# A routed mixture of experts behind attention: spreading the later lists' work over other hooks, and one-hot rows on GpSimd

## The chip, the cores and the metric

The kernel runs on one core of a Trainium2 chip. A core has five engines with an instruction stream each: TensorE (PE, matrix products and transposes), VectorE (DVE), ScalarE (ACT), GpSimd (POOL) and SyncE (SP, which here issues the loads). They share SBUF; products accumulate in PSUM, which has eight banks here. Every engine works through its own list in order and waits on semaphores for the others. The metric is the device time of one execution in microseconds (us).

## The reference

Eight batches of 544 tokens (512 local and 32 global) go through attention with 8 heads of 64, and the outputs of all heads are joined to rows of 512, which go through a mixture of 8 experts:

```python
mask = np.abs(pos[:, None] - pos[None, :]) <= 32
s_ll = np.where(mask, scale * q_l @ k_l.T, -1e9)         # a local token sees its window and the global ones
a_l = sm(np.concatenate([scale * q_l @ k_g.T, s_ll], axis=-1))
out_l = a_l @ np.concatenate([v_g, v_l])                 # a global token sees all
...
for b in range(B):
    prev_e = -1
    for s in range(S):
        fresh_e = int(np.argmax(logits[b, s]))
        if s == 0 or local_gate[b, s] < 0.5:
            e = fresh_e
        else:
            e = prev_e if prev_e >= 0 else fresh_e       # a token may keep its predecessor's expert
        prev_e = e
        p = softmax(logits[b, s])
        out[b, s] = p[e] * (np.maximum(x[b, s] @ w1[e], 0) @ w2[e])
```

w1 is 512x1024 and w2 1024x512 for each expert. Which tokens an expert gets is known only once the attention of all batches is done.

## The kernel before

**Two parts that overlap.** Attention runs unit by unit over the eight batches. Then come the expert blocks of up to 256 or more tokens. Three *early blocks* (0, 1, 2) take tokens of the first batches, whose lists are ready while the last three batches' attention and routing still run; eight *rem blocks* follow, one for each expert, each with a Switch over cases of its token count; then full blocks under an If. The early blocks are the place of this change.

**An early block** (`early`) is 24 steps: eight chunks of the first layer (`mm1`: 12 products of 128x256 by PE, then relu and high half hh by ACT, L1276, then the low half hl by DVE, L1279), then eight chunks of the second layer for the first 128 tokens (j0) and eight for the second (j1) (`mm2`: three products of 128x512 each, L1287). Matrices are split into a high and a low half of a rounded format, and a product is made of three: high by high, low by high, high by low. Three PSUM banks rotate among the chunks of `mm1` here: a chunk can start only once hh and hl have been made of the chunk that last used its bank.

**Hooks.** After each of the 24 steps `hook(i, k)` runs. It takes one step of the *tail*, a generator with what remains of attention and routing (`Attn.tail`): the last units' transposes and value products (`g_t`, `g_av`, `l_t`, `l_av`), the finishing pieces f1 to f4, the expert keys, the ranks and lists, `kinds` (which makes cnd, the case of each rem block), and `rest` (products and picks for the remaining lists). Then it flushes: the low halves of weight pieces that ACT has cast (L1183, by DVE, 128x1024). Then it splits as many further pieces as the table SP says for this hook (ACT's cast, L1173). A freed buffer starts the next load. So the order of the code is the order of the work on each engine, and the number of yields sets at which hook a step falls. `every(g, n)` puts n steps of g in one hook, `lag(n)` lets n hooks pass.

**Ranks and lists.** `rank1` compares tokens with experts (oh), makes prefix sums (pc), and lets PE count over partitions (L875 to L884, into PSUM). `place` makes counts, bases and limits from that. `rank2` makes a token's position, and splits it in a low part of seven bits (plo) and a high part. `low` (L916) makes, for some chunks of 128 tokens, rows of 128 that are one at a token's low part, by comparing an iota with plo. `pick` makes three DVE operations for each group (L1000, L1002, L1004, tile xT: one-hots of the high parts and their two multiples, called *products* below), and then PE multiplies the two one-hots over all 34 chunks (L1010) to get the lists of token numbers. Those feed the gathers (indirect DMAs by POOL, L1214), and the gathered rows are transposed (`xpose`: PE L1228, ACT L1230, DVE L1231).

**The hint.** Ahead of the fifth j0 chunk of block 2, `hint` makes every engine load cnd (L1487) to prepare the first rem block's branch.

The lines around the change:

```python
        for _ in range(SP[i][k]):        # hook: the pieces that are split here
            self.split()
...
            if mid and fc == 4:          # early block 2, second layer
                self.finish(True)
                while not self.known:
                    self.take(next(self.tail))
                self.hint(i + 1)
```

Of the kernel before, what the change touches and what calls it, by code (L numbers as in the profile page):

```python
# [8 lines left out]
F32 = mybir.dt.float32  # L9
# [4 lines left out]
ALU = mybir.AluOpType  # L14
AX = mybir.AxisListType
PSUM = bass.MemoryType.PSUM
ENGS = (mybir.EngineType.PE, mybir.EngineType.Activation, mybir.EngineType.DVE, mybir.EngineType.Pool, mybir.EngineType.SP)

P = 128
# [11 lines left out]
NT = 34  # L31
NA = 5
CA = 4 * NA + 1
# [23 lines left out]
RE = 2  # L57
# [13 lines left out]
def lag(n):  # L71
    for _ in range(n):
        yield


def every(g, n):
    for k, _ in enumerate(g):
        if k % n == n - 1:
            yield
# [22 lines left out]
class Attn:  # L102
# [431 lines left out]
    def tail(self, sg, sl, fin, rt, moe):  # L534
        b = B - 1
        fin = [x for x in fin if x[0] is not None]
        self.g_t(sg)
        yield
        self.g_av(sg)
        self.at2.close()  # L540
        moe.alloc_a()
        yield
        self.l_t(sl, 0)
        self.l_t(sl, 1)
        yield
        self.l_av(sl, 0)
        yield
        self.l_av(sl, 1)
        self.at1.close()
        moe.alloc_b()  # L550
        yield
        while fin:
            f, a = fin.pop(0)
            f(*a)
            yield
        self.f1g(b)
        yield
        self.f1(b, 3)
        yield
        self.f2g(b)  # L560
        yield
        self.f2(b)
        yield from lag(2)
        self.f3(b, rt, False)
        yield
        c = self.cur[b]
        yield from every(rt.keys(b, c["L"]), 2)
        yield
        yield from rt.stage_b(self.ps_t, self.ps_o, rt.probs(b, c["L"], c["xa"]))
        self.f4(b, rt)  # L570
        yield from every(rt.lists(self.ps_o), 2)
        yield LISTS
        yield from every(rt.kinds(), 3)
        yield KINDS
        yield from every(rt.rest(self.ps_o), RE)


class Consts:
# [22 lines left out]
class Route:  # L601
# [4 lines left out]
    def setup(self):  # L606
        nc, cst, c = self.nc, self.cst, self.pool
# [32 lines left out]
        self.pos = c.tile([P, NT], F32, name="pos")  # L640
        self.pi = c.tile([P, 2, NT], I32, name="pi")
        self.plo = c.tile([P, NT], BF16, name="plo")
        self.o1 = c.tile([P, NT, P], BF16, name="o1")
        self.oe = c.tile([P, CA, 2, 2 * NX], BF16, name="oe")
        self.idx = c.tile([P, 2 * NX + 4 * E + 2 * NR], I32, name="idx")
# [214 lines left out]
    def rank1(self, c0, c1, po, first):  # L860
        nc = self.nc
        n = c1 - c0
        bc = [P, E, n]
        oh = self.oh[:, :, c0:c1]
        nc.vector.tensor_tensor(out=oh, in0=self.io8.rearrange("p (e o) -> p e o", o=1).broadcast_to(bc), in1=self.ei[:, c0:c1].rearrange("p (o t) -> p o t", o=1).broadcast_to(bc), op=ALU.is_equal)
        yield
        pcf = self.pc.rearrange("p e t -> p (e t)")[:, 0:E * n]
        pc = pcf.rearrange("p (e t) -> p e t", t=n)
        yield from self.prefix(oh, pc, n)
        if first:  # L870
            nc.vector.tensor_copy(self.sumA, pc[:, :, n - 1])
            yield
        else:
            cp = po()
            nc.tensor.matmul(cp[:, 0:E], self.ones, self.sumA, start=True, stop=False, skip_group_check=True)  # L875
            nc.tensor.matmul(cp[:, 0:E], self.ones, pc[:, :, n - 1], start=False, stop=True, skip_group_check=True)
            self.cntp = cp[:, 0:E]
        yield PSUM
        rp = po()
        rpv = self.rpv = rp[:, 0:E * n].rearrange("p (e t) -> p e t", t=n)  # L880
        nc.tensor.matmul(rpv, self.nlt, oh, start=True, stop=False, skip_group_check=True)
        if not first:
            nc.tensor.matmul(rpv, self.ones, self.sumA.rearrange("p (e o) -> p e o", o=1).broadcast_to(bc), start=False, stop=False, skip_group_check=True)
        nc.tensor.matmul(rpv, self.ones, pc, start=False, stop=True, skip_group_check=True)  # L884

    def rank2(self, c0, c1):
        nc = self.nc
        n = c1 - c0
        oh = self.oh[:, :, c0:c1]
        rv = self.rv.rearrange("p e t -> p (e t)")[:, 0:E * n].rearrange("p (e t) -> p e t", t=n)  # L890
        nc.vector.tensor_tensor(out=rv, in0=self.rpv, in1=oh, op=ALU.mult)
        yield
        nc.vector.tensor_reduce(out=self.pos[:, c0:c1], in_=rv.rearrange("p e t -> p t e"), axis=AX.X, op=ALU.add)
        yield
        nc.vector.tensor_copy(self.pi[:, 0, c0:c1], self.pos[:, c0:c1])
        yield
        nc.vector.tensor_scalar(out=self.pi[:, 1, c0:c1], in0=self.pi[:, 0, c0:c1], scalar1=7, scalar2=None, op0=ALU.arith_shift_right)
        yield
        nc.vector.tensor_scalar(out=self.pi[:, 0, c0:c1], in0=self.pi[:, 0, c0:c1], scalar1=127, scalar2=None, op0=ALU.bitwise_and)
        yield  # L900
        nc.vector.tensor_copy(self.plo[:, c0:c1], self.pi[:, 0, c0:c1])
        yield

    def prefix(self, oh, pc, n):
# [111 lines left out]
    def lists(self, po):  # L1016
        nc = self.nc
        yield from self.place(self.cntp, NT, NX, NR)
        cid = self.tmp("cid", [P, 2 * E + NR, 2], BF16)
        cr = cid[:, 0:2 * E].rearrange("p (e a) j -> p e (a j)", a=2)  # L1020
        cf = cid[:, 2 * E:]
        rm = self.tmp("rm", [P, E], I32)
        nc.vector.tensor_scalar(out=rm, in0=self.cn, scalar1=255, scalar2=None, op0=ALU.bitwise_and)
        yield
        sh = self.tmp("sh", [P, E], F32)
        nc.vector.tensor_scalar(out=sh, in0=self.left, scalar1=0.0, scalar2=None, op0=ALU.is_ge)
        yield
        nc.vector.scalar_tensor_tensor(out=sh, in0=rm, scalar=float(P), in1=sh, op0=ALU.is_le, op1=ALU.mult)
        yield
        fb = self.tmp("fb", [P, E], F32)  # L1030
        nc.vector.scalar_tensor_tensor(out=fb, in0=self.nbc, scalar=-4.0, in1=sh, op0=ALU.add, op1=ALU.subtract)
        yield
        nc.vector.tensor_tensor(out=cr, in0=fb.rearrange("p (e o) -> p e o", o=1).broadcast_to([P, E, 4]),
                                in1=self.io8[:, 0:4].rearrange("p (o j) -> p o j", o=1).broadcast_to([P, E, 4]), op=ALU.add)
        yield
        nc.vector.scalar_tensor_tensor(out=cr[:, :, 0], in0=sh, scalar=4.0, in1=fb, op0=ALU.mult, op1=ALU.add)
        yield
        ge = self.ge[:, NX:]
        mf = self.tmp("mf", [P, NR, E], F32)
        nc.vector.tensor_tensor(out=mf, in0=ge[:, :, 0:E], in1=self.sd.rearrange("p (o e) -> p o e", o=1).broadcast_to([P, NR, E]), op=ALU.mult)  # L1040
        yield
        k3 = self.tmp("k3", [P, NR], F32)
        nc.vector.scalar_tensor_tensor(out=k3, in0=self.ek, scalar=2.0, in1=self.k2[:, 0:NR], op0=ALU.mult, op1=ALU.add)
        yield
        m3 = self.tmp("m3", [P, NR], F32)
        nc.vector.tensor_reduce(out=m3, in_=mf, axis=AX.X, op=ALU.add)
        yield
        yield from self.rank2(CA, NT)
        nc.vector.scalar_tensor_tensor(out=cf[:, :, 0], in0=k3, scalar=-2.0, in1=m3, op0=ALU.add, op1=ALU.add)
        yield  # L1050
        phi = self.tmp("phi", [P, NT], BF16)
        nc.vector.tensor_tensor(out=phi, in0=self.hi, in1=self.pi[:, 1], op=ALU.add)
        yield
        nc.vector.tensor_scalar(out=cf[:, :, 1], in0=cf[:, :, 0], scalar1=1.0, scalar2=None, op0=ALU.add)
        yield
        for c0 in range(CA, NT, 5):
            yield from self.low(c0, min(c0 + 5, NT))
        self.pk = (cid, phi)
        yield from self.pick(cid, phi, self.o2, 0, 4, 2 * NX, ((0, NT),), po, 16)

# [33 lines left out]
class Moe:  # L1094
# [216 lines left out]
    def hook(self, i, k):  # L1311
# [9 lines left out]
        if i == NX - 1:  # L1321
            self.finish()
        for _ in range(SP[i][k]):
            self.split()
# [204 lines left out]
def _sp(d):  # L1529
    return [d.get(k, 0) for k in range(24)]  # L1530


SP = [_sp({1: 1, 2: 1, 3: 1, 4: 1, 6: 1, 7: 1, 10: 1, 13: 1, 15: 1, 19: 1}),
      _sp({0: 1, 1: 1, 2: 1, 3: 1, 5: 1, 7: 1, 8: 1, 11: 1, 13: 1, 15: 1, 17: 1, 19: 1}),
      _sp({1: 1, 3: 1, 5: 1, 7: 1, 10: 1, 12: 1, 14: 1})]


@with_exitstack
# [83 lines left out]
```

## Time and profile before

| what | value |
|---|---|
| median of 3 runs | 685.71 us (684.99 to 685.96) |
| the profiled execution's time | 684.55 us |
| its span | 682.8 us, so 1.75 us lie around the span |
| granted TensorE clock, mean | 0.995 |
| busy: PE, DVE, ACT, POOL | 655.4, 433.7, 342.1, 195.0 us |
| the chain that ended last, PE's share | 56% |

A row of the timeline gives start, duration, engine, line, operation, tiles (output <- inputs, buffer numbers left out), shape, and a count where several follow each other; in brackets stands the idle time of the engine ahead of it and what ended that. A DVE row can reach over the start of the next (a low half starts at 307.21, lasts 1.22, and the next row starts at 308.35), so DVE work in a row is priced by the distance of its starts. The early blocks lie between about 229 and 322 us of the span; lines of `kernel.py` before the change are meant everywhere.

### The profile page before, as it was taken

What the parts mean: (1) busy time and instruction counts of PE and PEld (TensorE: products, weight loads), DVE (VectorE), ACT (ScalarE), POOL (GpSimd) and SP (SyncE); (2) the same over time, 40 slices, a digit from 0 to 9 for tenths busy, and PEclk for the clock granted to TensorE, in tenths of its full rate; (3) what the DMA queues carried; (4) which work ended last, traced back from release to release, by engine and by line L of the source; (5) the groups of instructions that cost most, each with busy time, mean ns of one, the idle gap of its engine ahead of it and who ended that gap; (6) DMA issues with size and microseconds to landing.
All of it is one profiled execution on the core that took longest, in us unless ns stands there. A gap on an engine that the chain in (4) does not pass through costs nothing.

```text
span 682.8 us, 18511 instructions
## 1 busy us (share of the span) xinstructions
PE 655.4 (96%) x7285; PEld 556.2 (81%) x7285; DVE 433.7 (64%) x1101; ACT 342.1 (50%) x614; POOL 195.0 (29%) x321
## 2 busy tenths in 40 slices
PE   8999999999999899998999899999999999999995
PEld 7778778777677787886987798989898989898994
DVE  7878778788887677988425553626374526355573
ACT  4555556555555574743427534435354425255563
POOL 7634334343324301031213304021123011133023
PEclk9999999999999999999999999999999999999998
DMA  8966967866757497766626674528283617265673
GB/s 321 405 217 249 336 216 305 316 247 237 303 188 291 135 353 255 259 206 200 254 89 223 212 246 151 183 82 265 86 297 120 235 63 236 93 218 182 222 276 102
DMA packets 42886, 151.47 MB, mean 222 GB/s; under 512 B 7837, under 2 KB 9117, under 8 KB 38560
## 3 DMA queue, kind: packets, MB, share of 16 engines
q1 hardware_dynamic: 35536, 126.92, 52.5%
q0 software_dynamic: 6832, 21.90, 9.5%
q8 instruction: 78, 1.28, 0.8%
q14 instruction: 152, 1.25, 0.6%
q10 hardware_dynamic: 288, 0.13, 0.1%
HBM read 130.55 MB, written 19.16 MB: 219 GB/s over the span
## 4 chain that ended last, share of the span: by engine, by line
PE 56%; DVE 6%; issue 1%; ACT 1%; POOL 0%; DVEq 0%; POOLq 0%; ACTq 0%
PE ps L1274 26%; PE ps L1287 23%; PE ps L1228 2%; PE ps L1293 2%; DVE wp L1183 1%; DVE wq L1183 1%; DVE xT L1002 0%; DVE xT L1000 0%; PE ps L1010 0%; DVE xl L1183 0%; ACT wp L1173 0%; DVE wp L1231 0%; POOL xa L1214 0%; DVE o L916 0%; DVE xl L1231 0%
## 5 line engine op out<-in xcount | busy, mean ns | idle before, releaser
L1306 POOL DMA_INDIRECT out_dram<-y,tk x39 | 40.8, 1045 | 309.5 <-ACT y L1305 221.7
L1287 PE MATMUL ps<-wp,wq 128*128 128x512 f32 x444 | 114.5, 403 | 1.0 <-ACT wq L1403 1.0
L1274 PE MATMUL ps<-wp,wp 128*128 128x256 f32 (+6 forms) x672 | 107.7, 320 | 0.0
L1274 PEld LDWEIGHTS ps<-wp,wp 128*128 128x128 f32 x672 | 103.5, 188 | 3.5
L1287 PEld LDWEIGHTS ps<-wp,wq 128*128 128x128 f32 x444 | 82.2, 190 | 18.1 <-ACT wq L1403 1.2
L1279 DVE SCALAR_TENSOR_TENSOR wq<-ps,wq 128x384 fp32r<-128x384 f32 (+4 forms) x112 | 43.5, 414 | 56.5 <-ACT wq L1276 48.0
L193 POOL TENSOR_SCALAR_AFFINE_SELECT qbd<-raw 64x512 f32<-64x512 f32 x62 | 44.3, 714 | 118.4 <-PE ps L246 92.2
L1276 ACT ACTIVATE wq<-ps 128x256 fp32r<-128x256 f32 (+6 forms) x80 | 36.9, 463 | 76.0 <-PE ps L1274 63.9
L246 PE MATMUL ps<-kx,qbd 128*64 128x128 f32 x1024 | 67.4, 275 | 1.3 <-issue 0.7
L1231 DVE TENSOR_TENSOR wp<-ps,wp 128x512 fp32r<-128x512 f32 x40 | 27.5, 691 | 58.3 <-ACT wp L1230 58.3
L257 ACT ACTIVATE pe<-pe 128x512 f32<-128x512 f32 x64 | 40.7, 636 | 43.8 <-DVE pe L253 43.8
L246 PEld LDWEIGHTS ps<-kx,qbd 128*64 128x64 f32 x1024 | 58.5, 138 | 2.1 <-POOL kx L193 1.1
L251 DVE TENSOR_REDUCE mx<-ps 128x4 f32<-128x512 f32 x64 | 43.8, 685 | 24.3 <-PE ps L246 24.1
L1183 DVE TENSOR_TENSOR wp<-raw,wp 128x1024 fp32r<-128x1024 f32 x47 | 57.0, 1217 | 2.9 <-ACT wp L1173 2.8
L1214 POOL DMA_INDIRECT xa<-xs,idx x42 | 50.2, 1194 | 18.8 <-issue 8.5
L1305 ACT ACTIVATE y<-ps,pp 128x512 f32<-128x512 f32 x35 | 24.2, 690 | 60.3 <-PE ps L1287 48.4
L1173 ACT CAST wp<-raw 128x1024 fp32r<-128x1024 f32 x49 | 50.9, 1047 | 1.3 <-ACT hh L1276 0.5
L1230 ACT CAST wp<-ps 128x512 fp32r<-128x512 f32 x40 | 23.5, 589 | 50.1 <-PE ps L1228 49.9
L253 DVE TENSOR_TENSOR pe<-ps,mx 128x512 f32<-128x512 f32 x64 | 44.0, 687 | 1.6
L279 PEld LDWEIGHTS ps<-v,pt 128*32 128x32 f32 x2048 | 33.1, 110 | 14.1 <-issue 7.9
L279 PE MATMUL ps<-v,pt 128*32 128x65 f32 x2048 | 41.7, 222 | 2.1 <-DVE xa L287 1.1
L193 POOL TENSOR_SCALAR_AFFINE_SELECT kx<-raw 128x384 f32<-128x384 f32 (+3 forms) x127 | 42.6, 368 | 3.1 <-DMA raw<-in_qk_dram 1.0
(296 smaller groups left out, 1188.2 us busy)
## 6 DMA issues: line engine op xcount, KB each, us to landing
raw<-in_w_dram SPq DMA_DIRECT2D x78, 512.0 KB, 4.4
v<-in_vw_dram SPq DMA_DIRECT2D x32, 1040.0 KB, 9.2
raw<-in_qk_dram SPq DMA_DIRECT2D x32, 528.0 KB, 7.8
xa<-in_w_dram SPq DMA_DIRECT2D x26, 512.0 KB, 4.2
xT<-in_w_dram SPq DMA_DIRECT2D x20, 512.0 KB, 5.1
xs<-xa SPq DMA_DIRECT2D x8, 1056.0 KB, 5.9
qgb<-in_qg_dram SPq DMA_DIRECT2D x8, 128.0 KB, 4.7
xa<-xs,idx POOLq DMA_INDIRECT x42
```

The costliest lines, as they stand in the source:

```text
L193: self.nc.gpsimd.affine_select(out=out, in_=in_, pattern=pat, compare_op=ALU.is_ge, fill=0.0, base=0, channel_multiplier=0)
L246: nc.tensor.matmul(sp[64 * t2:64 * t2 + 64, t], qbd[:, w], kf[:, f:f + P], start=False, stop=True, skip_group_check=True)
L251: nc.vector.tensor_reduce(out=mx, in_=st["sp"], axis=AX.X, op=ALU.max)
L253: nc.vector.tensor_tensor(out=st["pe"][:, 4 * hb:4 * hb + 4], in0=st["sp"], in1=mx.broadcast_to([P, 4, P]), op=ALU.subtract)
L279: nc.tensor.matmul(o[32 * w4:32 * w4 + 32, g, h], pt[:, 2 * g + w4 // 2, w4 % 2, h, :], v[:, w, h * (D + 1):(h + 1) * (D + 1)], start=True ...
L1173: nc.scalar.copy(out=hi, in_=raw)
L1183: (nc.gpsimd if pool else nc.vector).tensor_tensor(out=lo, in0=raw, in1=hi.bitcast(F32), op=ALU.subtract)
L1214: self.nc.gpsimd.indirect_dma_start(out=self.xr[j] if k == "early" else self.xr4[:, j], out_offset=None, in_=src, in_offset=bass.IndirectO ...
L1274: nc.tensor.matmul(ph, a[:, dc, fs], b_[:, dc, n0:n1], start=(n == 0), stop=(n == 11))
L1279: nc.vector.scalar_tensor_tensor(out=o[:, fc, c:c + b_ - a], in0=ph[:, a - n0:b_ - n0], scalar=0.0, in1=hh[:, fc, a:b_].bitcast(F32), op0= ...
L1287: nc.tensor.matmul(py, a[:, fc, js], b_[:, fs], start=(fc == 0 and k == 0), stop=(fc == 7 and k == 2))
L1306: sc = nc.gpsimd.indirect_dma_start(out=self.out, out_offset=bass.IndirectOffsetOnAxis(ap=tk[rows, js], axis=0), in_=y[rows], in_offset=No ...
```

## The change

1. In the tail, `g_av` comes two hooks after `g_t` (one before), and `l_t` in the same hook as `g_av`. The table SP of block 0 splits the pieces at hooks 2, 3, 4, 5, 6, 7 where it was 1, 2, 3, 4, 6, 7.
2. The second call of `rank1` lets six steps more pass before PE's count products. The steps are taken three to a hook here, so the products, and all routing behind them, come two hooks later, in block 1.
3. The low one-hot rows of the last 13 chunks, three DVE operations of five, five and three chunks, become 13 GpSimd operations, each on one chunk with a scalar of float32 (tile plf, to which DVE now casts). They are all issued in one step.
4. `rest` is started inside `kinds`: each of its three hooks takes one of the products too, so that the first group's three products stand ahead of cnd. By the other edits the pick of L1010 comes one chunk later.
5. SP of block 2 lost its entry at hook 14, so one piece is left to the rem blocks.

```diff
         self.g_t(sg)
-        yield
+        yield from lag(2)
         self.g_av(sg)
         self.at2.close()
         moe.alloc_a()
-        yield
         self.l_t(sl, 0)
...
         yield LISTS
-        yield from every(rt.kinds(), 3)
+        r = rt.rest(self.ps_o)
+        for _ in every(rt.kinds(), 3):
+            next(r)
+            yield
         yield KINDS
-        yield from every(rt.rest(self.ps_o), RE)
+        yield from every(r, RE)
...
+        self.plf = c.tile([P, NT - CA], F32, name="plf")
...
         else:
+            yield from lag(6)
             cp = po()
...
-        nc.vector.tensor_copy(self.plo[:, c0:c1], self.pi[:, 0, c0:c1])
+        nc.vector.tensor_copy(self.plo[:, c0:c1] if c0 < CA else self.plf[:, 0:c1 - c0], self.pi[:, 0, c0:c1])
...
-        for c0 in range(CA, NT, 5):
-            yield from self.low(c0, min(c0 + 5, NT))
+        for c0 in range(CA, NT):
+            nc.gpsimd.tensor_scalar(out=self.o1[:, c0], in0=self.io128, scalar1=self.plf[:, c0 - CA:c0 - CA + 1], scalar2=None, op0=ALU.is_equal)
+        yield
...
-SP = [_sp({1: 1, 2: 1, 3: 1, 4: 1, 6: 1, 7: 1, 10: 1, 13: 1, 15: 1, 19: 1}),
+SP = [_sp({2: 1, 3: 1, 4: 1, 5: 1, 6: 1, 7: 1, 10: 1, 13: 1, 15: 1, 19: 1}),
       _sp({0: 1, 1: 1, 2: 1, 3: 1, 5: 1, 7: 1, 8: 1, 11: 1, 13: 1, 15: 1, 17: 1, 19: 1}),
-      _sp({1: 1, 3: 1, 5: 1, 7: 1, 10: 1, 12: 1, 14: 1})]
+      _sp({1: 1, 3: 1, 5: 1, 7: 1, 10: 1, 12: 1})]
```

In the order of the instructions this shows at three places (lines of the change are up to five higher: L1274 is L1279 there, L1183 is L1188). The first is PE in block 0, its first chunks: L342 is g_av, L263 is l_t, wp_101 the weight piece of chunks 2 and 3. Before:

```order
L1274 MATMUL ps_66<-xl,wp_100 128x256 x4
L342 MATMUL ps_69<-v_132,ptg_151 32x65 x2
...
L342 MATMUL ps_69<-v_133,ptg_151 32x65 x2
L1274 MATMUL ps_63<-xh,wp_101 128x256 x8
L1274 MATMUL ps_63<-xl,wp_101 128x256 x4
L263 MATMUL ps_67<-idf,pe_138 128x128 x4
```

And in the change:

```order
L1279 MATMUL ps_66<-xl,wp_100 128x256 x4
L1279 MATMUL ps_63<-xh,wp_101 128x256 x8
L1279 MATMUL ps_63<-xl,wp_101 128x256 x4
L342 MATMUL ps_69<-v_132,ptg_151 32x65 x2
...
L342 MATMUL ps_69<-v_133,ptg_151 32x65 x2
L263 MATMUL ps_67<-idf,pe_138 128x128 x4
```

g_av's 24 rows of products went from ahead of chunk 2 to behind it. On DVE, just after, the low half of the third piece (wp_4271 before, wp_4286 now) went from between two hl to behind l_av's three operations (rs, rs, xa); before:

```order
L1279 SCALAR_TENSOR_TENSOR hl<-ps_63,hh 128x256
L1183 TENSOR_TENSOR wp_4271<-raw_79,wp_4271 128x1024
L1279 SCALAR_TENSOR_TENSOR hl<-ps_65,hh 128x256
L282 TENSOR_SCALAR rs_123<-ps_70 128x4
L284 RECIPROCAL rs_123<-rs_123 128x4
L287 TENSOR_TENSOR xa_109<-ps_70,rs_123 128x2x128
```

```order
L1284 SCALAR_TENSOR_TENSOR hl<-ps_65,hh 128x256
L282 TENSOR_SCALAR rs_123<-ps_70 128x4
L284 RECIPROCAL rs_123<-rs_123 128x4
L287 TENSOR_TENSOR xa_109<-ps_70,rs_123 128x2x128
L1188 TENSOR_TENSOR wp_4286<-raw_79,wp_4286 128x1024
```

The second place is DVE at the end of block 1, from phi and cid (the high parts and what they are compared with) to the first products. Before:

```order
L1052 TENSOR_TENSOR phi<-hi,pi 128x34
L1054 TENSOR_SCALAR cid<-cid 128x13
L916 TENSOR_TENSOR o_292<-io_263,plo 128x640 x2
L1183 TENSOR_TENSOR wq_4378<-raw_80,wq_4378 128x1024
L916 TENSOR_TENSOR o_292<-io_263,plo 128x384
L1000 TENSOR_TENSOR xT<-cid,phi 128x34x4
```

And in the change, of DVE and then of POOL:

```order
L1056 TENSOR_TENSOR phi<-hi,pi 128x34
L1058 TENSOR_SCALAR cid<-cid 128x13
L1004 TENSOR_TENSOR xT<-cid,phi 128x34x4
L1188 TENSOR_TENSOR wq_4377<-xa_108,wq_4377 128x1024
```

```order
L1311 DMA out_dram<-y_4380,tk_96 4352x512
L1061 TENSOR_SCALAR o_293<-io_263,plf 128x128 x13
L1311 DMA out_dram<-y_4378,tk_96 4352x512
L1219 DMA xa_108<-xs,idx 128x528 x4
```

The one-hots left DVE, and stand on POOL between the two output stores of block 1. The third place is DVE ahead of cnd in block 2, from about the hl of chunk 7 on (kq, kb, kt: small operations of `kinds`). Before:

```order
L1279 SCALAR_TENSOR_TENSOR hl<-ps_66,hh 128x256
L1078 TENSOR_SCALAR kb<-kq 1x8
L1081 TENSOR_SCALAR kt<-kq 1x8
L1083 TENSOR_TENSOR kt<-kt,kb 1x8
L1085 SCALAR_TENSOR_TENSOR kt<-left,kt 1x8
L1087 TENSOR_TENSOR cnd<-kt,kb 1x8
L1183 TENSOR_TENSOR wp_4272<-raw_79,wp_4272 128x1024
L1000 TENSOR_TENSOR xT<-cid,phi 128x9x54
```

And in the change:

```order
L1006 TENSOR_TENSOR xT<-xT,t_266 128x9x54
L1083 TENSOR_SCALAR kb<-kq 1x8
L1086 TENSOR_SCALAR kt<-kq 1x8
L1088 TENSOR_TENSOR kt<-kt,kb 1x8
L1008 TENSOR_SCALAR xT<-xT,ipf 128x9x54
L1188 TENSOR_TENSOR wp_4287<-raw_79,wp_4287 128x1024
L1090 SCALAR_TENSOR_TENSOR kt<-left,kt 1x8
L1092 TENSOR_TENSOR cnd<-kt,kb 1x8
```

The first group's products, and a low half, went from behind cnd to ahead of it.

## The prediction

> **What bounds the kernel now.** I read the busy times first:
>
> ```profile
> PE 655.4 (96%) x7285; PEld 556.2 (81%) x7285; DVE 433.7 (64%) x1101; ACT 342.1 (50%) x614; POOL 195.0 (29%) x321
> ```
>
> TensorE (PE) is busy for 655.4 of the span's 682.8 us. The change removes no PE product, so it can only move PE's waits. These I took from the waits grouped by what ended them (place, releaser: us, count, longest). The five that lie where the change works are:
>
> ```profile
> PE ps L1228 <- DVE wp L1231: 2.2, 1, 2.2
> PE ps L1274 <- DVE hl L1279: 1.7, 1, 1.7
> PE ps L342 <- ACT ptg L332: 1.7, 1, 1.7
> PE ps L876 <- DVE pc L911: 1.1, 1, 1.1
> PE ps L1287 <- ACT wp L1173: 0.7, 1, 0.7
> ```
>
> Together they are 7.4 us, and each edit aims at one of them. The last is labelled with a cast, but the hint's register load of cnd stands in PE's order just there. The table by stretches (length; busy time of PE, its weight loads, VectorE (DVE), ACT, POOL; clock, DMA share, GB/s) shows what else is scarce:
>
> ```profile
> 279.00:289.00 10.00, 10.00 (x49) 8.14 (x48) 9.79 (x32) 8.45 (x11) 0.98 (x1) 1.00 0.82 293
> 289.00:299.00 10.00, 8.33 (x87) 7.76 (x86) 9.46 (x17) 3.29 (x7) 2.53 (x1) 1.00 0.78 238
> ```
>
> In the second stretch PE is busy for 8.33 us and DVE for 9.46: the end of early block 1 and the start of block 2 are DVE's. GpSimd (POOL) is nearly free there.
>
> **A. g_av one hook later.** The rows of PE, POOL, ACT and DVE around it, then the chain that ended last:
>
> ```profile
> 235.27 0.93 PE L342 MATMUL ps<-v,ptg 128*32 128x65 f32 x48 [1.66 <-ACT ptg L332]
> 237.08 0.74 PE L1274 MATMUL ps<-xh,wp 128*128 128x256 f32 x4 [0.20 <-POOL wp L1183]
> 234.65 2.37 POOL L1183 TENSOR_TENSOR wp<-raw,wp 128x1024 fp32r<-128x1024 f32 x1 [4.37 <-DVE gx L785]
> 238.77 1.07 ACT L265 COPY pt<-ps 128x512 f32<-128x512 f32 x2
> 239.73 1.06 ACT L1173 CAST wp<-raw 128x1024 fp32r<-128x1024 f32 x1
> 241.10 0.42 DVE L1279 SCALAR_TENSOR_TENSOR hl<-ps,hh 128x256 fp32r<-128x256 f32 x1 [0.80 <-ACT hh L1276]
> 242.19 1.22 DVE L1183 TENSOR_TENSOR wp<-raw,wp 128x1024 fp32r<-128x1024 f32 x1
> 238.30 0.87 PE ps L263 x8
> 239.17 1.41 PE ps L1274 x12
> 240.58 0.59 PE ps L279 x32
> 241.18 1.63 PE ps L1274 x12
> ```
>
> The 1.66 us before g_av would be filled by chunk 2 of block 0. But chunk 2's second four products need the low half that GpSimd finishes at 234.65+2.37=237.02 in either order, and in the old order PE waits only 0.20 for it. So chunk 2 ends at about 238.2 as before, and g_av's 0.87 (235.27 to the next chunk's 236.14) now comes behind it: +0.87.
>
> Then the split of piece 2 goes from hook 1 to hook 2, behind l_t's copies on ACT. The copies start at 238.77+0.87, so the cast runs from 240.60 to 241.66. On DVE the hl of chunk 3 comes at 241.97, l_av's three small operations stand between it and the piece's low half (the row spacing 241.10 to 242.19 is 1.09), and the low half runs from 243.06 to 244.28. Chunk 4 waits for it before its second four products; these and the four behind them take about 0.95, so the chunk ends at 245.2, where it ended at 241.18+1.63=242.81. **A = +2.4** (bounds +0.87, if the low half gets in ahead of l_av's operations, to +2.6).
>
> **B and C. The later count products, and the one-hots.** PE's 1.10 us at L876 goes: it now does chunk 0 of block 1 first. But the gain meets DVE:
>
> ```profile
> 274.24 0.42 DVE L1279 SCALAR_TENSOR_TENSOR hl<-ps,hh 128x256 fp32r<-128x256 f32 x1
> 290.01 1.55 DVE L916 TENSOR_TENSOR o<-io,plo 128x640 bf16<-128x640 bf16 x2
> 291.48 1.22 DVE L1183 TENSOR_TENSOR wq<-raw,wq 128x1024 fp32r<-128x1024 f32 x1
> 292.61 0.56 DVE L916 TENSOR_TENSOR o<-io,plo 128x384 bf16<-128x384 bf16 x1
> 293.08 0.29 DVE L1000 TENSOR_TENSOR xT<-cid,phi 128x136 bf16<-128x136 bf16 x1
> 296.21 1.08 DVE L1279 SCALAR_TENSOR_TENSOR hl<-ps,hh 128x256 fp32r<-128x256 f32 x3
> 296.68 1.22 PE L1274 MATMUL ps<-xh,wp 128*128 128x256 f32 x8 [1.67 <-DVE hl L1279]
> ```
>
> From 274.57, the row behind the first one, DVE runs without an idle row until block 2's first hl at 296.21, 21.64 us, and PE waits for that hl. The three one-hot operations give back 291.48-290.01=1.47 and 293.08-292.61=0.47, together 1.94. The two hooks' delay puts four or five small operations (L785, cn, f2, nbc, bs; 0.1 to 0.2 each) behind 274.24 that ran ahead of it: about 0.75. The chain is then 20.45 long and starts about 0.5 earlier, so the first hl comes 1.94-0.75+0.5=1.7 earlier.
>
> Against that stands GpSimd's work beside DVE. No 128x128 tensor_scalar is in the trace; the nearest rows, and what GpSimd's own low halves do to DVE, are:
>
> ```profile
> L193 POOL TENSOR_SCALAR_AFFINE_SELECT kx<-raw 128x128 f32<-128x128 f32 x32 | 9.6, 299 | 3.1 <-DMA raw<-in_qk_dram 1.0
> L665 POOL IOTA i<- 128x128 int32 x1 | 0.2, 240 | 0.0
> 227.91 2.37 POOL L1183 TENSOR_TENSOR wp<-raw,wp 128x1024 fp32r<-128x1024 f32 x1
> 227.33 2.98 DVE L751 TENSOR_TENSOR lvm<-sk,lvm 128x5 f32<-128x5 f32 x1
> 234.89 0.42 DVE L1279 SCALAR_TENSOR_TENSOR hl<-ps,hh 128x256 fp32r<-128x256 f32 x1 [0.29 <-ACT hh L1276]
> ```
>
> A DVE operation of 128x5 took 2.98 us and ended with the GpSimd operation that ran beside it (227.33+2.98=230.31, 227.91+2.37=230.28): with two inputs in SBUF it was held for the whole of it. The hl at 234.89, with one input in PSUM, took its usual 0.42 during another such operation. [...]
>
> Between the cast of plf and the hl stand eight DVE operations of the kind that can be held (three low halves, phi, cid, three xT). I let each wait for one GpSimd operation, at 0.25 from the two rows above: 2.0. The bounds are 0.5 (most meet no operation) and 13x0.28=3.6 (DVE held by all thirteen). [...] **B + C = -1.7+2.0 = +0.3.**
>
> **D. cnd.** The hint makes PE load cnd from SBUF ahead of the fifth second-layer chunk of block 2, at the same place in both orders.
>
> ```profile
> 304.11 0.42 DVE L1279 SCALAR_TENSOR_TENSOR hl<-ps,hh 128x256 fp32r<-128x256 f32 x1 [0.63 <-ACT hh L1276]
> 307.12 0.16 DVE L1087 TENSOR_TENSOR cnd<-kt,kb 1x8 int32<-1x8 f32 x1
> 307.21 1.22 DVE L1183 TENSOR_TENSOR wp<-raw,wp 128x1024 fp32r<-128x1024 f32 x1
> 308.35 0.66 DVE L1000 TENSOR_TENSOR xT<-cid,phi 128x486 bf16<-128x486 bf16 x1
> 310.02 0.65 DVE L1000 TENSOR_TENSOR xT<-cid,phi 128x486 bf16<-128x486 bf16 x1
> 308.52 0.72 PE L1287 MATMUL ps<-wq,hh 128*128 128x512 f32 x2 [0.68 <-ACT wp L1173]
> ```
>
> Before, cnd is done at 307.28 and PE comes at 307.84, so the load by itself costs 0.68. From the hl of chunk 6 (304.11) to cnd DVE has no idle row. The change puts more into this stretch: the three small operations eid, eoh and the first of cnd, now behind that hl (about 0.35), the first three xT products (310.02-308.35=1.67), and one more low half (308.35-307.21=1.14). cnd is then done 3.16 later on the same clock, at 310.44, and PE goes on at 310.44+0.68=311.12 in place of 308.52. **D = +2.6** (0 if cnd is in time after all, 3.2 at most).
>
> **E. The next gather's transposes.**
>
> ```profile
> 318.75 0.66 PE L1228 MATMUL ps<-idf,xa 128*128 128x128 f32 x4 [2.23 <-DVE wp L1231]
> 318.01 1.28 DVE L1231 TENSOR_TENSOR wp<-ps,wp 128x512 fp32r<-128x512 f32 x2
> ```
>
> PE waited 2.23 for L1231, which on DVE ran behind the products and low halves that followed cnd. From cnd's end to 318.01 these were 10.73 us. Now a group of three products (1.67) and a low half (1.14) are ahead of cnd, and another (1.14) is left to the next block, since SP[2] has lost its last entry: 6.8 remain, L1231 starts at 310.44+6.8=317.2 and its first is done by 318.0, while PE, 2.6 later, needs it at 319.1. **E = -2.2.**
>
> **F. One weight piece less ahead** in the eight blocks that follow costs nothing: the next block's first pieces are cast some 8 us before PE reads them, and the moved low half finds DVE idle there (64% busy over the span). If that cover is gone it costs one low half, 1.2, so I keep ±1.2 in the range.
>
> **Sum:** 2.4+0.3+2.6-2.2 = **+3.1**. The profiled execution took 684.55 us, 1.75 of it around the span; 684.55+3.1=687.65. The median of the timed runs, 685.71, stands 1.16 above it, so I say **688.8**.
>
> **The rivals.** I call a difference of 0.2% (1.4 us) the least that can be told from no change.
>
> *GpSimd holds DVE for all thirteen operations* (c=3.6 for 2.0): +4.7, 690.4. [...]
>
> *No change.* DVE gets in between GpSimd's operations (c=0.5) and the piece's low half in A is early enough (A=0.87): 0.87-1.2+2.6-2.2=+0.1, about 685.8. For it: the 0.42 us of hl beside GpSimd, and that A and c are my least known terms.
>
> *Faster by a part.* cnd also comes in time (D=0), as when the DVE work shifts with its earlier start: 0.87-1.2+0-2.2=-2.5, 683.2. For it: PE's order at the hint is unchanged. Against: 3.16 us of work stand newly ahead of cnd.
>
> *All four waits go and none comes:* 2.23+1.67+1.66+1.10=6.7 less, 679.0. [...]
>
> **How the numbers follow.** The forecast has 0.42; its own range is 687.2 to 690.0 (A at its low bound, or c at its own, takes 1.5 off; F's 1.2 is on the other side). Full holding has 0.11, no change 0.25, the partial gain 0.15 and the full gain 0.07. So faster is 0.22, same 0.25 and slower 0.53. The range reaches from 683.3 to 690.6: it leaves out the full gain, half of the partial one and a little of the full holding.
>
> **What would show it.** Right: the wait before g_av is gone and one of over 1 us stands before chunk 4's second four products (L1274 behind the low half); the wait of 1.10 at L876 is gone; DVE's low halves and xT products beside the thirteen GpSimd operations last longer than 1.22 and 0.30; the wait at the hint is about 3 us where it was 0.68; that at L1228 is gone. Wrong: GpSimd's operations at half of 0.25 us or less, an hl x3 row over 1.5 us earlier against PE, cnd done before PE comes for it, or a new wait in the blocks behind, where I count none.

## The result: 8.1 us slower

The changed kernel takes 693.93 us (median of 6 runs, 692.09 to 695.99) against 685.84 us before; the ratio is 1.0125, with a 95% interval of 1.0106 to 1.0144. The forecast was slower, 688.8, and the time lies beyond the range's end of 690.6. In the profiled execution of the change the span is 691.9 us, 9.1 longer than before. Its busy times:

```profile
PE 661.1 (96%) x7285; PEld 559.6 (81%) x7285; DVE 431.0 (62%) x1097; ACT 340.8 (49%) x613; POOL 208.7 (30%) x334
```

PE has the same 7285 products and is busy 5.7 us longer: some of the time is not waiting but slower multiplying. The waits of PE, grouped by releaser, in the change (L1279 is the first layer, L1284 hl, L1188 the low halves, L1014 the pick, L1061 the new one-hots, L1292 the second layer; numbers up to five above those of before):

```profile
PE ps L1292 <- DVE xT L1004: 3.2, 1, 3.2
PE ps L1014 <- POOL o L1061: 2.3, 6, 0.4
PE ps L1279 <- POOL wp L1188: 2.1, 2, 1.7
...
PE ps L1279 <- DVE wp L1188: 1.7, 1, 1.7
...
PE ps L1279 <- ACT wp L1178: 1.0, 1, 1.0
...
PE ps L1279 <- DVE hl L1284: 0.5, 1, 0.5
```

The waits of 2.2 at L1228, 1.7 at L342 and 1.1 at L876 are gone, and that of 1.7 for hl is 0.5. In their place stand 3.2 at the hint (0.7 before), 2.3 in the pick, and the three about chunks 2 and 4 of block 0 (2.1, 1.7 and 1.0). To see what each place is worth, I set the start of the same PE instruction in the two timelines side by side; the last column is what the stretch behind the row above added.

| same instruction of PE | before, us | change, us | later by | added there |
|---|---|---|---|---|
| chunk 0 of block 0 | 229.17 | 229.96 | 0.79 | 0.79 |
| chunk 3 | 238.93 | 240.60 | 1.67 | +0.88: g_av |
| behind chunk 4 | 242.74 | 246.33 | 3.59 | +1.92: the low half behind l_av |
| chunk 6 | 245.22 | 250.32 | 5.10 | +1.51: slower products |
| chunk 1 of block 1 | 268.37 | 272.14 | 3.77 | -1.33: L876's wait |
| chunk 0 of block 2 | 290.54 | 294.92 | 4.38 | +0.61 |
| chunk 3 | 296.68 | 299.85 | 3.17 | -1.21: hl's wait |
| chunk 5, behind the pick | 300.61 | 306.78 | 6.17 | +3.00: the pick |
| first second-layer chunk | 304.93 | 312.58 | 7.65 | +1.48: slower products |
| behind the hint | 308.52 | 318.70 | 10.18 | +2.53: cnd |
| first transposes, L1228 | 313.40 | 325.09 | 11.69 | +1.51: slower products |
| third transposes | 318.75 | 328.05 | 9.30 | -2.39: L1228's wait |
| end of the span | 682.8 | 691.9 | 9.1 | -0.2 |

**The pick.** On PE in the change, the last one-hots come one by one:

```profile
302.69 0.86 PE L1014 MATMUL ps<-xT,o 128*128 128x8 bf16 x28
303.85 0.18 PE L1014 MATMUL ps<-xT,o 128*128 128x8 bf16 x1 [0.30 <-POOL o L1061]
...
306.74 0.18 PE L1014 MATMUL ps<-xT,o 128*128 128x8 bf16 x1 [0.40 <-POOL o L1061]
306.78 1.17 PE L1279 MATMUL ps<-xh,wp 128*128 128x256 f32 x8
```

The pick lasted 0.86 before (298.23 to 299.09) and lasts 4.09 here. The line's own view and single operations of GpSimd from the timeline:

```profile
L1061 POOL TENSOR_SCALAR o<-io,plf x13: 597/599/1781, 295.1 to 306.1; 128x128 bf16<-128x128 bf16 x13
295.09 1.62 POOL L1061 TENSOR_SCALAR o<-io,plf 128x128 bf16<-128x128 bf16 x1 [3.62 <-DVE cid L1053]
296.70 1.78 POOL L1061 TENSOR_SCALAR o<-io,plf 128x128 bf16<-128x128 bf16 x1
299.91 0.60 POOL L1061 TENSOR_SCALAR o<-io,plf 128x128 bf16<-128x128 bf16 x1
```

and of DVE in the same time:

```profile
294.98 1.22 DVE L1188 TENSOR_TENSOR wq<-raw,wq 128x1024 fp32r<-128x1024 f32 x1
296.11 0.18 DVE L1056 TENSOR_TENSOR phi<-hi,pi 128x34 bf16<-128x34 f32 x1
...
296.60 1.21 DVE L1188 TENSOR_TENSOR wq<-xa,wq 128x1024 fp32r<-128x1024 f32 x1
```

An operation takes 0.60 us by itself, more than twice the 0.25 I priced it at. The one that starts at 295.09, just after a low half, ends at 296.71, that is 0.60 after DVE has gone on to its next row at 296.11; the next one waits likewise for the low half of 296.60 and ends 0.7 after it. So here DVE holds GpSimd, not the other way: DVE's low halves kept 1.21 to 1.22 us. Four of the thirteen were held, for about 1.0 each, and all thirteen took 11.6.

**The slower products.** The table by stretches, PE alone (length, busy time, products, granted clock, DMA share, GB/s), in steps of 3.41 us that I put on the clock's own changes:

```profile
243.43:246.84 3.41, 1.74 (x41) 0.99 0.34 87
246.84:250.25 3.41, 3.41 (x27) 0.51 0.91 264
...
304.86:308.27 3.41, 2.06 (x17) 1.00 0.00 0
308.27:311.69 3.42, 3.42 (x19) 0.51 0.83 289
315.10:318.51 3.41, 0.39 (x2) 1.00 0.67 240
318.51:321.93 3.42, 3.23 (x8) 0.51 0.40 146
```

Behind each of three of the new waits (chunk 4, the pick, the hint) the granted clock is half for one step of 3.41 us, which costs 1.5 us each time, 4.5 together: half of the whole loss. In each of the two executions all changes of the clock lie on one grid of 3.413 us (in the change the half steps begin at 246.84, 308.27, 318.51, 386.78 and 687.15 us, that is 18, 3, 20 and 88 such steps apart), and each run of half steps follows a grid step in which PE was busy for little (0.39, 1.74 and 2.06 of 3.41 us here). Before, the blocks up to 330 us have no half step in the profiled execution. But they do have a thinly filled step, and the one behind it is not at half:

```profile
293.44:296.86 3.42, 1.75 (x15) 1.00 0.83 244
296.86:300.27 3.41, 3.41 (x56) 1.00 0.49 163
```

So a thin step came ahead of each fall of the clock, but not every thin step brings one. On the grids of these two profiles, the steps at full clock with up to 1.37 us of PE's work had a half step behind them (in the change 0.39, 1.09 and 1.25, before 1.37 and one without work at 675.73). Of those with 1.59 to 2.06 two had one (1.74 and 2.06) and five had none (1.59 and 1.92 in the change; 1.75 twice and 2.00 before), and none with 2.22 or more had one. What decides between 1.59 and 2.06 stays open.

### The profile page after: what moved, and what is told of

Its sections match the earlier page's. It is cut to its first block, busy times and chain, and to the rows that moved or that the text cites. A ratio compares the mean times of both kernels' runs of the same rounds, so it can differ in the third digit from the quotient of the medians.

```text
span 691.9 us, 18504 instructions
## 1 busy us (share of the span) xinstructions
PE 661.1 (96%) x7285; PEld 559.6 (81%) x7285; DVE 431.0 (62%) x1097; ACT 340.8 (49%) x613; POOL 208.7 (30%) x334
## 3 DMA queue, kind: packets, MB, share of 16 engines
q14 instruction: 152, 1.25, 0.5%
## 4 chain that ended last, share of the span: by engine, by line
PE 56%; DVE 4%; POOL 1%; DMA 1%; issue 1%; ACT 1%; SPq 1%; POOLq 0%; ACTq 0%
PE ps L1292 25%; PE ps L1279 24%; PE ps L1233 2%; PE ps L1298 2%; DVE wp L1188 1%; POOL o L1061 1%; DMA raw<-in_w_dram 1%; DVE wq L1188 1%; SPq L420 0%; DMA xs<-xg 0%; PE ps L1417 0%; ACT wp L1178 0%; DVE hl L1284 0%; POOL xa L1219 0%; DVE xl L1236 0%
## 5 line engine op out<-in xcount | busy, mean ns | idle before, releaser
L1292 PE MATMUL ps<-wp,wq 128*128 128x512 f32 x444 | 114.2, 402 | 1.0 <-ACT wq L1408 1.0
L1279 PE MATMUL ps<-wp,wp 128*128 128x256 f32 (+6 forms) x672 | 107.7, 320 | 0.0
L1279 PEld LDWEIGHTS ps<-wp,wp 128*128 128x128 f32 x672 | 103.4, 188 | 3.5
L1292 PEld LDWEIGHTS ps<-wp,wq 128*128 128x128 f32 x444 | 82.3, 191 | 18.2 <-ACT wq L1408 1.2
L1284 DVE SCALAR_TENSOR_TENSOR wq<-ps,wq 128x384 fp32r<-128x384 f32 (+4 forms) x112 | 43.2, 412 | 56.9 <-ACT wq L1281 54.9
L1219 POOL DMA_INDIRECT xa<-xs,idx x42 | 52.5, 1249 | 14.5 <-issue 9.8
L1188 DVE TENSOR_TENSOR wp<-raw,wp 128x1024 fp32r<-128x1024 f32 x38 | 46.0, 1215 | 2.8 <-ACT wp L1178 2.8
L1178 ACT CAST wp<-raw 128x1024 fp32r<-128x1024 f32 x40 | 41.4, 1046 | 3.5 <-DVE xT L1004 3.5
```

The source lines that it names most:

```text
L1178: nc.scalar.copy(out=hi, in_=raw)
L1188: (nc.gpsimd if pool else nc.vector).tensor_tensor(out=lo, in0=raw, in1=hi.bitcast(F32), op=ALU.subtract)
L1219: self.nc.gpsimd.indirect_dma_start(out=self.xr[j] if k == "early" else self.xr4[:, j], out_offset=None, in_=src, in_offset=bass.IndirectO ...
L1279: nc.tensor.matmul(ph, a[:, dc, fs], b_[:, dc, n0:n1], start=(n == 0), stop=(n == 11))
L1284: nc.vector.scalar_tensor_tensor(out=o[:, fc, c:c + b_ - a], in0=ph[:, a - n0:b_ - n0], scalar=0.0, in1=hh[:, fc, a:b_].bitcast(F32), op0= ...
L1292: nc.tensor.matmul(py, a[:, fc, js], b_[:, fs], start=(fc == 0 and k == 0), stop=(fc == 7 and k == 2))
```

## The experiments

The runs were made in three sets, each on a chip of its own with the kernel before beside it (684.52, 685.75 and 685.68 us; 685.84 is that of the result). So kernels of different sets are compared by their ratios to it. The expectations are as they were written ahead of the runs. The second part was not undone by itself.

**Part 1 undone.**

```diff
-        yield from lag(2)
+        yield
         self.g_av(sg)
...
+        yield
         self.l_t(sl, 0)
...
-SP = [_sp({2: 1, 3: 1, 4: 1, 5: 1, 6: 1, 7: 1, 10: 1, 13: 1, 15: 1, 19: 1}),
+SP = [_sp({1: 1, 2: 1, 3: 1, 4: 1, 6: 1, 7: 1, 10: 1, 13: 1, 15: 1, 19: 1}),
```

> The changed kernel with its first part undone (g_av one hook after g_t, l_t a hook later, block 0 splits at hooks 1, 2, 3, 4, 6, 7). Theory: of the 8.1 us lost, the first part holds 2.8 in waits (0.9 at chunk 2, 1.9 at chunk 4) and 1.5 in the half-speed stretch of TensorE's clock that follows the wait at chunk 4 (246.9 to 250.3 us): 4.3 less, about 689.6 us, with two half-speed stretches left between 290 and 330 us. Rival: the half-speed stretches do not come from the waits, so only the waits come back: about 691.1 us, and three stretches in all stay between 229 and 330 us.

Measured: 687.75, a ratio of 1.0050 (1.0031 to 1.0069). So part 1 was worth about 4.7 of the 8.1 us. The new waits at chunks 2 and 4 are gone and so is the half-speed step behind them; this profile has one step between 229 and 330 us, behind the pick (from 301.11 us, at 0.51, behind a step with 1.35 us of work), and none behind the hint, whose wait is as long as ever (3.3). There the wait was shared by two steps of the grid, with 1.52 and 2.03 us of work. The same wait can thus have a half step behind it or not. The time fits the theory (a ratio of 1.0055) and not the rival (1.0077), though one half step more went than the theory had.

**Part 3 undone on the engine alone.**

```diff
-        nc.vector.tensor_copy(self.plo[:, c0:c1] if c0 < CA else self.plf[:, 0:c1 - c0], self.pi[:, 0, c0:c1])
+        nc.vector.tensor_copy(self.plo[:, c0:c1], self.pi[:, 0, c0:c1])
...
-        for c0 in range(CA, NT):
-            nc.gpsimd.tensor_scalar(out=self.o1[:, c0], in0=self.io128, scalar1=self.plf[:, c0 - CA:c0 - CA + 1], scalar2=None, op0=ALU.is_equal)
+        for c0 in range(CA, NT, 5):
+            all_(self.low(c0, min(c0 + 5, NT)))
         yield
```

> The changed kernel with its third part undone on the engine alone: the low one-hots of the last 13 chunks are three DVE operations again, issued in the same one step. Theory: GpSimd is held by DVE and not DVE by GpSimd, and PE waits in the pick for the last one-hots: the pick's wait (3.0) and the half-speed stretch behind it (1.5) go, and DVE's first hl of block 2 comes 1.2 to 1.9 later against PE (L1284's wait 1.7 to 2.4 in place of 0.5): about 690.6 us. Rival, of the prediction: GpSimd's operations hold DVE for about 2 us, which then come back: hl's wait stays at 0.5 and the time is about 689.4 us.

Measured: 687.92, a ratio of 1.0044 (1.0025 to 1.0063). The wait in the pick is gone, and hl's is what the theory said:

```profile
PE ps L1279 <- DVE hl L1284: 2.4, 1, 2.4
```

The rival, that GpSimd had held DVE and hl would stay at 0.5, is refuted by this wait. By the time alone it would not be: the ratio, put on the result's 685.84, gives 688.9, nearer to the rival's 689.4 than to the theory's 690.6. The time at half clock was 10 us in the mean of these runs, where it was 20 in the change's, so more of it went than the one half step that the theory counted. This profile also bears on the clock. It has part 1 with the same 1.67 us wait at chunk 4 as the change:

```profile
243.85 0.74 PE L1279 MATMUL ps<-xh,wp 128*128 128x256 f32 x4 [1.67 <-DVE wp L1188]
```

but here the grid of 3.41 us lies so that the wait is shared by two steps:

```profile
239.63:243.04 3.41, 2.55 (x47) 1.00 0.94 342
243.04:246.45 3.41, 2.60 (x47) 1.00 0.30 103
246.45:249.87 3.42, 3.42 (x32) 1.00 0.91 308
```

Each step holds 2.55 or more of work, and the clock stays whole. In the change the whole wait lay in one step (1.74 of work), and the next was at half. So the wait's length alone does not decide. That its share in one step of the grid does, a grid that differs from execution to execution, fits this pair, but the step with 1.75 us of before, without a half step behind it, shows that the share is not all of it.

**Part 4 undone.**

```diff
-        r = rt.rest(self.ps_o)
-        for _ in every(rt.kinds(), 3):
-            next(r)
-            yield
+        yield from every(rt.kinds(), 3)
         yield KINDS
-        yield from every(r, RE)
+        yield from every(rt.rest(self.ps_o), RE)
```

> The changed kernel with its fourth part undone: the first three products stand behind cnd again. Theory: cnd is done 1.67 earlier, so the hint's wait falls from 3.2 to about 1.6 and the half-speed stretch behind it (1.5) goes, but L1236 does not come earlier, so about 2 us of the wait at L1233 return: net 1.1 less, about 692.8 us. Rival: the products ahead of cnd cost the whole 2.5 of the hint and the stretch, and buy nothing: about 689.9 us.

Measured: 688.72, a ratio of 1.0068 (1.0046 to 1.0090), 4.2 above the kernel before on that chip: part 4 was worth about 3.4 to 4. The hint's wait fell by 1.1, to

```profile
PE ps L1289 <- DVE xT L1001: 2.1, 1, 2.1
```

and no wait came back at the transposes (L1228 of before), so my theory fell there: the products ahead of cnd bought nothing. Even with the products behind cnd, DVE had been idle for 0.56 us when it could start the transposes' low half; the first row is this run's, the second the change's:

```profile
322.30 0.69 DVE L1233 TENSOR_TENSOR wp<-ps,wp 128x512 fp32r<-128x512 f32 x1 [0.56 <-ACT wp L1232]
326.34 0.69 DVE L1236 TENSOR_TENSOR wp<-ps,wp 128x512 fp32r<-128x512 f32 x1 [2.14 <-ACT wp L1235]
```

The rest of the gain goes with the clock: over its ten runs the time at half clock, read from the mean granted clock, was 14 us in the mean where it was 20 in the change's six. But the profiled execution still has three half steps between 229 and 330 us, one of them behind the hint's shorter wait (from 314.5 us, at 0.50, behind a step with 1.38 us of work), so the theory's condition for 1.5 of its gain did not hold there.

By the ratios, undoing part 1, 3 or 4 gains 4.7, 5.1 and 3.4 us. Together that is more than the whole loss, so these worths do not add up. The time at half clock fell in each of the three (from 20 us to 15, 10 and 14), and these falls may overlap; no run here separates them.

**Part 5 alone, on the kernel before, in two sets.**

```diff
-      _sp({1: 1, 3: 1, 5: 1, 7: 1, 10: 1, 12: 1, 14: 1})]
+      _sp({1: 1, 3: 1, 5: 1, 7: 1, 10: 1, 12: 1})]
```

> The kernel before with the fifth part alone: block 2 splits one piece less (none at hook 14). Theory: one low half (1.14) less stands on DVE ahead of L1231, so the wait of 2.2 at L1228 falls to 1.1, and the blocks behind do not pay: about 684.7 us, 1.1 less. Rival: the piece is missed later, in a rem block, and the time stays at 685.8 or goes up to 687.

> The kernel before with the fifth part alone, once more, beside the next two on one chip. By its waits (L1228's fell from 2.2 to 1.1) it should be 1.1 us faster, a ratio of 0.9984; the run before gave 0.9951 with 2 us less of half-speed clock than its partner had by chance. Theory: a ratio between 0.995 and 0.998. Rival: no difference, 1.000.

Measured: 681.50, a ratio of 0.9951 (0.9934 to 0.9968), and in the other set 684.35, 0.9968 (0.9948 to 0.9987). The wait is half of what it was:

```profile
PE ps L1228 <- DVE wp L1231: 1.1, 1, 1.1
```

and no rem block waits for the piece that it now makes itself. This part is a gain of 0.3 to 0.5%, hidden in the change by the others. The waits explain 1.1 us of it, about the 1.3 of the second set; the first set's further 2 us go with less time at half clock (7.0 us in the mean against 11.7 of its partner).

**The price of the GpSimd operation**, with 20 operations added in the first rem block of the kernel before; nobody reads what they write.

```diff
+                for n in range(8):
+                    nc.gpsimd.tensor_scalar(out=self.rt.o1[:, n], in0=self.rt.io128, scalar1=self.rt.pos[:, n:n + 1], scalar2=None, op0=ALU.is_equal)
+                for n in range(8):
+                    nc.gpsimd.tensor_scalar(out=self.rt.o1[:, n + 8], in0=self.rt.io128, scalar1=5.0, scalar2=None, op0=ALU.is_equal)
...
```

> The kernel before with 20 GpSimd operations added in the first rem block, behind block 3's gathers and writing one-hot rows that nobody reads any more: eight of 128x128 with a scalar from SBUF, eight of 128x128 with a constant, four of 128x512 with a scalar from SBUF. It measures the price by itself. Theory: 128x128 takes 0.60 us wherever DVE runs nothing with two SBUF inputs, about 1.6 where it runs a low half (GpSimd waits until that is over), and DVE's low halves stay at 1.22; most of the 0.60 is a fixed price, so 128x512 takes about 0.9 to 1.1. Rival: GpSimd's time goes by elements (128x512 about 2.4), or the scalar read from SBUF is what costs (a constant gives 0.3). Rival of the prediction: low halves beside these operations last longer than 1.22.

The views of the three lines (min/median/max in ns):

```profile
L1469 POOL TENSOR_SCALAR o<-io,pos x8: 590/596/1485, 368.5 to 373.5; 128x128 bf16<-128x128 bf16 x8
L1471 POOL TENSOR_SCALAR o<-io x8: 526/527/1400, 375.0 to 381.5; 128x128 bf16<-128x128 bf16 x8
L1473 POOL TENSOR_SCALAR o<-io,pos x4: 1556/1559/1563, 382.2 to 386.8; 128x512 bf16<-128x512 bf16 x4
```

0.60 undisturbed, as expected; a constant saves only 0.07. But 128x512 takes 1.56, between theory (at most 1.1) and rival (2.4): from the two sizes, (1.56-0.60)/384=2.5 ns go to each element of a row, and 0.28 us would be fixed. The maxima (1.40, 1.49) are again those beside low halves. The kernel's own time, 694.5 in one run, is not used: PE waited 7.5 us in the next block, for ACT's part of the transposes (L1230).

This profile also has the order that the prediction feared, a low half that starts just behind one of these operations:

```profile
371.58 0.59 POOL L1469 TENSOR_SCALAR o<-io,pos 128x128 bf16<-128x128 bf16 x1
371.65 1.37 DVE L1183 TENSOR_TENSOR wp<-xT,wp 128x1024 fp32r<-128x1024 f32 x1
```

Held to the end of the operation, the low half would have taken 1.74 us; it took 1.37, that is 0.15 more than the usual 1.22. The rival of the prediction is thus right by 0.15 for one low half; the others kept 1.21 to 1.22.

**Part 3 alone, on the kernel before.**

```diff
+        self.plf = c.tile([P, NT - CA], F32, name="plf")
...
-        nc.vector.tensor_copy(self.plo[:, c0:c1], self.pi[:, 0, c0:c1])
+        nc.vector.tensor_copy(self.plo[:, c0:c1] if c0 < CA else self.plf[:, 0:c1 - c0], self.pi[:, 0, c0:c1])
...
-        for c0 in range(CA, NT, 5):
-            yield from self.low(c0, min(c0 + 5, NT))
+        for c0 in range(CA, NT):
+            nc.gpsimd.tensor_scalar(out=self.o1[:, c0], in0=self.io128, scalar1=self.plf[:, c0 - CA:c0 - CA + 1], scalar2=None, op0=ALU.is_equal)
+        yield
```

> The kernel before with the third part alone: the 13 one-hots on GpSimd in one step. Theory: the 13 operations take 13x0.6 plus about four waits of 1.0 for DVE's low halves, 11.8 us from the cast of plf at 288.7; the pick stands one hook earlier than before, so PE waits in it until about 300.7 and loses 3.4, with 1.5 more where a half-speed stretch follows: about 688 to 689.5 against 684.5 for the kernel before. Rival: DVE is held by GpSimd (hl's wait of 1.7 stays or grows) and PE does not wait in the pick: 684.5 to 686.

Measured: 689.38, a ratio of 1.0059 (1.0038 to 1.0079). As the theory had it: hl's wait is gone, and PE waits in the pick for nine one-hots.

```profile
PE ps L1011 <- POOL o L1058: 3.5, 9, 0.4
```

**Eight of the thirteen on GpSimd, with part 5.**

```diff
+        if c0:
+            nc.vector.tensor_copy(self.plf, self.pi[:, 0, CA + 5:NT])
...
-        for c0 in range(CA, NT, 5):
-            yield from self.low(c0, min(c0 + 5, NT))
+        for c0 in range(CA + 5, NT):
+            nc.gpsimd.tensor_scalar(out=self.o1[:, c0], in0=self.io128, scalar1=self.plf[:, c0 - CA - 5:c0 - CA - 4], scalar2=None, op0=ALU.is_equal)
+        yield from self.low(CA, CA + 5)
+        yield from lag(2)
...
-      _sp({1: 1, 3: 1, 5: 1, 7: 1, 10: 1, 12: 1, 14: 1})]
+      _sp({1: 1, 3: 1, 5: 1, 7: 1, 10: 1, 12: 1})]
```

> The kernel before with the fifth part (no split at hook 14 of block 2) and only the last eight of the 13 one-hots on GpSimd, at the same hooks as before. Theory: GpSimd is done by 8x0.6 plus about four waits of 1.0, 8.8 us after the cast, 297.5 and so before the pick needs the last rows; DVE's chain is 1.1 shorter, so hl's wait falls from 1.7 to 0.6: 1.1 less than the fifth part alone, a ratio of about 0.9935 to the kernel before. Rival: GpSimd holds DVE (hl's wait stays at 1.7): the ratio of the fifth part alone, 0.995.

Measured: 683.56, a ratio of 0.9977 (0.9961 to 0.9992): no better than part 5 alone. hl's wait fell as expected, but the pick took it back, since the eight operations lasted 10.2 us and not 8.8 (of the DVE low halves beside them two stood in a row, at 292.23 and 293.37):

```profile
PE ps L1013 <- POOL o L1060: 0.8, 2, 0.4
PE ps L1279 <- DVE hl L1284: 0.7, 1, 0.7
```

**Half of part 2 on top of that, and without GpSimd.** In both, `yield from lag(3)` stands ahead of the count products; the second makes the one-hots by DVE in one hook.

> The same, with half of the second part: rank1's count products one hook later (three steps more), and the one-hots in one hook in place of two, so that kinds and picks stay where they were. Theory: the wait of 1.1 at L876 goes, and about 0.4 of small DVE operations move into the chain ahead of hl: 0.7 less than without it, a ratio of about 0.9925. Rival: DVE's chain sets block 2's start, so the 1.1 gained before it is lost again at hl (its wait grows to 1.7): no difference.

> The kernel before with the fifth part, the count products one hook later (three steps more), and the three DVE one-hot operations in one hook, so that kinds and picks stay where they were; nothing is on GpSimd. Theory: the wait of 1.1 at L876 goes, but DVE's chain to block 2's first hl is as long as it was, so hl's wait grows from 1.7 to about 2.5: no more than 0.3 less than the fifth part alone. Rival: the 1.1 are gained.

Measured: 683.39, 0.9968 (0.9943 to 0.9993), and 684.47, 0.9981 (0.9958 to 1.0004). Neither can be told from its partner without the lag (0.9977 and 0.9968). In the second 0.4 of the wait for pc stayed, and hl's went from 1.7 to

```profile
PE ps L1276 <- DVE hl L1281: 1.8, 1, 1.8
```

so the 0.7 gained at the count products is not told from noise, and the theory's loss at hl (to about 2.5) did not come either. What half of part 2 is worth stays open within some 0.2%.

**Two pieces less in block 2.**

```diff
-      _sp({1: 1, 3: 1, 5: 1, 7: 1, 10: 1, 12: 1, 14: 1})]
+      _sp({1: 1, 3: 1, 5: 1, 7: 1, 10: 1})]
```

> The kernel before with block 2 splitting two pieces less (none at hooks 12 and 14). Theory: the rest of the wait at L1228 (1.1) goes, and the first rem block makes its pieces a step later without TensorE waiting for one: 1.1 less than the fifth part alone. Rival: the cover of the rem blocks is gone by the second piece, and PE waits there for a cast or a low half by 1 us or more: no gain over the fifth part, or a loss.

Measured: 682.66, a ratio of 0.9947 (0.9929 to 0.9965), where part 5 alone had 0.9968 in the same set. The wait at L1228 in block 2 is gone and the rem blocks show no new one. It is 0.5% below the kernel before; that it is faster than part 5 alone is not clear of noise, since the two intervals overlap.

## Why the prediction was wrong, point by point

- **That it gets slower, since new waits take the place of those that go:** right. The sum of the terms was 3.1 and measured 8.5. Of the 5.4 between, 4.5 are the clock, 0.8 are B + C, 0.4 are A, and D and E make it 0.3 less.
- **A, g_av and the low half, +2.4:** right in its mechanism, a little above its bound of 2.6; 0.88+1.92=2.80. Chunk 2 did end no earlier, g_av's 0.9 came on top, and chunk 4 waited 1.67 for the low half behind l_av's operations.
- **B + C, +0.3:** a step that failed in its mechanism; that its size came out near, -1.33+0.61-1.21+3.00=+1.07, is luck, since two errors largely cancel (2.0 of holding that did not come, 3.0 in the pick that was no term). The chain of DVE was read rightly: without contention I had -1.7, and the places of L876's and hl's waits, with the 0.61 lost between them, give -1.93. But the price and the direction of the contention were wrong. I let GpSimd hold DVE for 2.0 us at 0.25 an operation. No run shows this 2.0: of the DVE operations beside the thirteen only cid was longer, by 0.09 us (0.27 for 0.18); it was DVE that held GpSimd, and an operation costs 0.60. I took the rows of affine_select (0.30) and iota (0.24) as near enough for a comparison, and they were not. The row in which GpSimd held DVE (the 2.98 us) was beside a GpSimd operation with two large inputs, and had begun 0.58 us ahead of it, so it did not show what a comparison does to DVE. And I asked what the new work does to DVE, but not when PE needs its result: 13 operations of 0.60 and four holds of 1.0 end 8 us behind what I assumed, in the pick, +3.0. The rival on holding had the wrong sign; none of the rivals had the pick. The case is shown by undoing part 3 (the pick's wait goes) and by part 3 alone (it comes).
- **D, cnd, +2.6:** right; 2.53. **E, -2.2:** right in size, -2.39. Part 4 was not needed for it: with the products behind cnd again, the wait at the transposes stayed away too. **F, nothing:** right, and shown by part 5 alone.
- **What was no term at all, and the step that failed by its size:** half of the loss, 4.5 us in the profiled execution, is PE's clock at half for 3.41 us behind each of three new waits. I read the column of the clock as 1.00 in the early blocks, took it for fixed, and added waits up as if each cost its length. This term alone decides: with 4.5 us less, by estimate, the change's 693.9 would be 689.4, inside the range. Over the runs the time at half clock was 20 us in the mean for the change and 8 to 12 for the kernel before in the three sets, so it is no accident of the profile. In the profiles of the kernel before and of the change a step of the grid with 2.06 us of work or less comes ahead of every fall of the clock; no share of work is a clean limit: a step with 2.06 us of work had a half step behind it, while before the change steps with 1.75 (293.44 to 296.86) and 2.00 (317.34 to 320.75) had none. That the new waits bring the half steps rests on this order in the traces; no run changed the clock alone.

With the measured terms the sum closes: 2.80-1.33+0.61-1.21+3.00+2.53-2.39+4.50 = 8.5, with 0.8 from before the change's place and -0.2 behind it, 9.1 of 9.1.

## What to carry to other kernels

Work that is moved to a free engine is priced from a row of the same operation, and then followed to its reader: 13 operations on an idle engine are free only if their last one ends before the waiting engine needs it. Where DVE ran its low halves of 1.22 us nearly back to back in the change, each of four held a GpSimd operation for about 1.0 us. A new wait of PE can cost more than its length, here 1.5 us more when a half step followed, so a sum of waits needs a term for the clock, with a range; and the plain lever here was to issue less ahead of a full DVE (two pieces left to the blocks behind: 0.5%).

## What the runs showed of the hardware

- A GpSimd comparison of 128x128 (bf16, scalar from SBUF) took 0.60 us, with a constant 0.53, of 128x512 1.56. One that started behind a DVE low half of 1.22 ended some 0.5 to 0.7 after it and lasted 1.5 to 1.8 in the change, while the low halves of DVE kept 1.21 to 1.22 there. In the other order, a low half that started beside the last 0.2 us of a GpSimd operation (298.24 us in the change) was not lengthened (1.22), and one that started 0.07 us behind the start of such an operation took 1.37 (the kernel with the added operations).
- PE's granted clock halved for whole steps of 3.413 us (0.51 from 246.84 to 250.25 us in the change), on a grid that was fixed within an execution (129 steps from 246.84 to 687.15 us) and differed between executions (half steps began at 386.78 us in the change and at 378.78 before, 2.3 steps apart). The same wait of 1.67 us at the same instruction had a half step behind it with 1.74 us of work in its grid step, and none where the grid split it into 2.55 and 2.60. But a step with 1.75 before the change had none either, so the work in a step does not settle it alone.
